# Two attention pairs of the second batch mixed as a couple, with X turned by the transfer queue

## The chip, the cores and the metric

One core of one Trainium2 chip runs the whole kernel. The metric is the device time of one execution in microseconds (us). Engines are named as in the profile: PE is TensorE (matmuls; PEld are its weight loads), DVE is VectorE, ACT is ScalarE, POOL is GpSimd, SP is SyncE, whose work here is to issue transfers in its program order.

## What is computed

Cosine attention, then a mixer that works across the sequence, then two dense layers. q, k and v have 8 batches, 12 heads, 448 positions and 64 values for each head.

```python
q_n = q / (norm(q) + 1e-6)
k_n = k / (norm(k) + 1e-6)
attn = softmax(q_n @ k_n.T / tau)
x = attn @ v                          # as (batch, 448, 768)
u = x + V.T @ (U.T @ x)               # U: 448 x 32, V: 32 x 448, over positions
out = u + relu(u @ w_ch1) @ w_ch2     # 768 -> 3072 -> 768
```

## The kernel before

**Pairs and stages.** Two heads make a pair: 6 pairs for each batch (`NP` = 6), 48 in all, counted through. Pair 10 and 11 are the last two of batch 1, pair 12 the first of batch 2. For each pair the kernel does these steps:

- Norms: q and k of a group of two pairs are loaded, squared on POOL (L243), summed on DVE (L248), rooted on ACT (L253, L254), inverted on DVE (L260, L262), and scaled to bf16 on POOL (L268).
- T: q and k are turned so that the 64 values lie on partitions. Up to pair 11 TensorE does it (`pe_T`, L297), and DVE copies the result (L302). From pair 12 on (`by_dma`, L281) SP's queue does it with a DMA transpose (L312).
- S: scores in four chunks of k's positions. Chunks 0 to 2 fill two banks each (L328), the last one half of that (L321, or `step_S3` at L332, which does the last chunks of two pairs at once). ACT takes the exponential (L350, L353).
- V: the product with v and a column of ones, in two halves (L373, L380), and the division on DVE (`divide_V`, L391, L392), which leaves X in bf16.
- Mixing: U.T X is added up over the positions, then multiplied with V, and X is added. Its result is one chunk of 128 rows of uE (even batches) or uO (odd ones), turned so that the dense layers can read it.

**Two forms of the mixing.** The one-pair form is `step_A` and `step_H`: four matmuls against U (L413) and an ACT copy (L419); four matmuls of X against the identity, which turn X into a PSUM bank (`pe_XT`, L427); one matmul of 448 columns with V (L438) into the same bank; and a DVE copy to uO or uE (L443). The couple form is used for two pairs at once. `step_XT` (L455) turns X by a DMA transpose on SP's queue as soon as it is divided. `step_A2` (L460) does both pairs' sums over U with eight matmuls of 32 columns each (L466) and one ACT copy (L470). `step_H2` (L474) multiplies with V in four matmuls of 64x64 (L480), and two DVE additions (L485) put the turned X on top. After the last pair of an odd batch, DVE copies 64 columns of uE to the end of uO (L450 or L488).

The couple form needs V on all four quarters of the partitions. `load_copies` (L159) and `place_copies` (L164) see to that, on POOL.

**Fill.** The dense layers of the batch before are cut into pieces of six matmuls: `steps_m1` (L510, 24 pieces, then a relu on ACT or DVE, L514 and L516) and `steps_m2` (L537; every four pieces one output chunk, evicted by L551, L553 or L555 and written by L561, L565). They stand in the list `fill`, and are put between the attention steps.

**The order.** Pairs 0 to 5 follow a list written out by hand (L625). From pair 6 on a loop (L791) goes over pairs n. For each, `order` lists attention steps with weights, and `spread` (L775) emits a step, then what `after` holds for that index, then its share of the fill. The dictionary `after` places the steps of the norms of later groups (L733 to L757), the loads, the DMA transposes and `place_copies`. A planner's costs (`est`) only choose ACT or DVE for some evictions. Each engine executes its instructions in the order in which they were emitted.

Pairs up to `FIRST2` = 2 * NP = 12 use the first pair of orders (L800 to L821): V of pair n - 1, then `A` and `Hs` of pair n - 1. Five pieces of fill go with each pair, and the pair that begins a batch (n = 12) gets all the rest. Then the dense layers of the batch just mixed are put into `fill`. Later pairs use the second orders (L839 to L871): V and the X transfer of pair n - 1, `A2` of a couple at the even pair after it, `H2` at the odd pair after that. Three pieces (`KEEP`) are held back from the pair that begins a batch, and run behind that `H2`.

PSUM has one bank each under the tags `ps_av` and `ps_x`. In `step_V` (L398) the second half goes to `ps_x` for pairs for which `by_dma` holds, and to `ps_av` otherwise; TensorE's turning of q and k also uses `ps_x`. For pair 12's group the squares are emitted at (9, 6) and (10, 0), sums at (10, 1) and (10, 3), the root at (10, 4), inversion and scaling at (10, 5); the numbers are pair n and index in its order.

Of the kernel before, what the change touches and what calls it, by code (L numbers as in the profile page):

```python
# [22 lines left out]
def kernel(  # L23
# [23 lines left out]
    NP = H // 2  # L47
# [233 lines left out]
    def by_dma(n):  # L281

        return n >= 2 * NP

    tp_of, sc_of = {}, {}

    def new_qkT(b, p):
# [44 lines left out]
    def step_S3(b, p):  # L332

        for i, (nm, tag) in enumerate((("av", "ps_av"), ("up", "ps_x"))):
            t = qkT[(b, p + i)]
            bank = psum.tile([128, 512], FP, name=nm, tag=tag, bufs=1)
            sc_of[(b, p + i, 3)] = bank.unsqueeze(1)
            for h in range(2):
                r, o = slice(64 * h, 64 * h + 64), 64 * (h ^ i)
                nc.tensor.matmul(out=bank[o:o + 64, 0:S], lhsT=t[r, 1, 384 + o:448 + o],  # L340
                                 rhs=t[r, 0, 0:S], start=True, stop=True)
        est.pe(0.19)
        for i in range(2):
            exp_S(b, p + i, 3)

    def exp_S(b, p, c):
        e = E[(b * NP + p) % 2]
        sc = sc_of.pop((b, p, c))
        if c == 3:
            nc.scalar.activation(out=last_of(b, p)[:, 0:S], in_=sc[:, 0, 0:S], func=AF.Exp)  # L350
            est.act(0.56)
        else:
            nc.scalar.activation(out=e[:, 2 * c:2 * c + 2, 0:S], in_=sc[:, :, 0:S], func=AF.Exp)  # L353
            est.act(0.93)

    def step_S(b, p, cs):
        for c in cs:
            pe_S(b, p, c)
            exp_S(b, p, c)
# [27 lines left out]
    def divide_V(b, p, half):  # L387
        X = X_of[(b, p)]
        av = av_of[(b, p, half)][:, 0:4 * (D + 1)].rearrange("p (i h d) -> p i h d", i=2, h=2)
        rd = work.tile([128, 4, 1], FP, name="rd", tag="rd", bufs=2)  # L390
        nc.vector.reciprocal(out=rd, in_=av.rearrange("p i h d -> p (i h) d")[:, :, D:D + 1])  # L391
        nc.vector.tensor_mul(  # L392
            X[:, 2 * half:2 * half + 2, :].rearrange("p i (h d) -> p i h d", h=2),
            av[:, :, :, 0:D],
            rd.rearrange("p (i h) o -> p i h o", h=2).to_broadcast([128, 2, 2, D]))
        est.dve(0.6)

    def step_V(b, p, half):  # L398
        if half == 1 and by_dma(b * NP + p):
            bank = psum.tile([128, 512], FP, name="up", tag="ps_x", bufs=1)  # L400
        else:
            bank = psum.tile([128, 512], FP, name="av", tag="ps_av", bufs=1)
        pe_V(b, p, half, bank)
        divide_V(b, p, half)
# [172 lines left out]
    pairs = [(b, p) for b in range(B) for p in range(NP)]  # L577
# [9 lines left out]
    def load_all(gi):  # L587
        if gi < len(groups):
            for x in ("q", "k", "v"):
                load(gi, x, nc.sync)  # L590
# [13 lines left out]
    def T(n):  # L604
        step_T(*pairs[n])

    def Sc(n, *cs):
        step_S(*pairs[n], cs)
# [121 lines left out]
    def put(n, at, fn):  # L730
        after.setdefault((n, at), []).append(fn)

    for gi in range(5, len(groups)):  # L733
        m, g = first_pair[gi], preps[gi]
        if m == NP + 2:
            at = [(NP, 1), (NP, 2), (NP + 1, 6), (NP, 5), (NP + 1, 0), (NP + 1, 1)]
            when = (NP + 1, 2)
        elif m == NP + 4:
            at = [(NP + 2, 0), (NP + 2, 1), (NP + 2, 6), (NP + 2, 4), (NP + 2, 6), (NP + 2, 7)]
            when = (NP + 3, 0)  # L740
        elif m == 2 * NP:
            at = [(m - 3, 6), (m - 2, 0), (m - 1, 0)] + [(m - 2, i) for i in (1, 3, 4)]
            when = (m - 2, 5)
        elif m == 2 * NP + 2:
            at = [(m - 2, i) for i in (0, 0, 6, 3, 4, 5)]
            when = (m - 2, 6)
        else:
            at = [(m - 3, 0), (m - 3, 0), (m - 3, 5)] + [(m - 2, i) for i in (0, 1, 2)]
            when = (m - 2, 3)

        put(*at[0], lambda g=g: g.square(0))
        put(*at[1], lambda g=g: g.square(1))
        put(*at[2], lambda g=g: g.values())
        put(*at[3], lambda g=g: g.reduce(0))
        put(*at[4], lambda g=g: g.reduce(1))
        put(*at[5], lambda g=g: g.root())
        put(*when, lambda g=g: (g.invert(), [g.scale(i, j, P_) for j in (0, 1) for i in (1, 0)]))  # L757
        if gi > 5 and m - 6 <= NP:
            put(*((NP, 3), (NP + 3, 0))[gi - 6], lambda gi=gi: load_all(gi))
        elif gi > 5:  # L760
            at = {2 * NP + 2: [(m - 4, 5), (m - 4, 6), (m - 3, 2)],
                  2 * NP + 4: [(m - 4, i) for i in (0, 2, 4)]}.get(m, [(m - 6, 4), (m - 5, 5), (m - 4, 3)])
            for x, w in zip("qkv", at):
                put(*w, lambda gi=gi, x=x: load(gi, x, nc.sync))
        if by_dma(m):
            put(m - 1, -1, lambda m=m: T(m))
            put(m - 1, 0, lambda m=m: T(m + 1))
# [2 lines left out]
    put(NP, 3, lambda: (load_w2(0, 0, 12), load_w2(0, 12, 24)))  # L770
    put(NP + 1, 2, lambda: (load_w2(1, 0, 12), load_w2(1, 12, 24)))
    put(NP + 3, 0, load_copies)
    put(NP + 5, 6, place_copies)

    def spread(n, order, nf, first=0):  # L775

# [9 lines left out]
            f(min(want - given, len(fill)))  # L786
            given = want

    FIRST2 = 2 * NP
    KEEP = 3  # L790
    for n in range(NP, NPAIR + 1):  # L791
        b, p = pairs[n] if n < NPAIR else (B, 0)
        now, nxt = n < NPAIR, n + 1 < NPAIR
        done = n > NP
        late = n > FIRST2
        for g in after.pop((n, -1), []):
            g()
        state_of["busy"] = n == NP + 1
        if not late:
            if n % 2 == 0:  # L800

                order = [
                    (1, lambda: Sc(n, 0, 1)),
                    (0, done and (lambda: V(n - 1, 0))),
                    (1, None if by_dma(n + 1) else (lambda: T(n + 1))),
                    (0, lambda: Sc(n, 3)),
                    (1, (lambda: V(n - 1, 1)) if done else None),
                    (0, done and (lambda: A(n - 1))),
                    (1, lambda: (Sc(n, 2), Sc(n + 1, 0))),
                    (1, (lambda: Hs(n - 1)) if done else None),  # L810
                ]
            else:
                order = [
                    (1, lambda: Sc(n, 1, 2)),
                    (1, lambda: V(n - 1, 0)),
                    (0, lambda: Sc(n, 3)),
                    (1, lambda: V(n - 1, 1)),
                    (1, not by_dma(n + 1) and (lambda: T(n + 1))),
                    (1, lambda: A(n - 1)),
                    (0, lambda: Hs(n - 1)),  # L820
                ]  # L821
            last = p == 0 and done
            nf = len(fill) if last else 5
            spread(n, order, nf)
            if last:
                f(len(fill))
                fill.extend(steps_m1(b - 1) + steps_m2(b - 1))
            continue

        def X2(m):  # L830
            step_XT(*pairs[m])

        def A2(m):
            step_A2(*pairs[m])

        def H2(m):
            step_H2(*pairs[m])

        if n % 2 == 0:  # L839
            order = [  # L840
                (2, now and (lambda: (step_S3(*pairs[n]), Sc(n, 0, 1)))),
                (2, lambda: V(n - 1, 0)),
                (2, lambda: (V(n - 1, 1), X2(n - 1))),
                (2, None),
                (3, lambda: (A2(n - 2), now and (Sc(n, 2), Sc(n + 1, 0)))),
                (2, not now and (lambda: H2(n - 2))),
            ]
            nf = len(fill) if not now else int(round((len(fill) - KEEP) / (1 + (-p) % NP)))
            spread(n, order, nf)
            if not now:  # L850
                f(len(fill))
                fill.extend(steps_m1(b - 1) + steps_m2(b - 1))
            continue
        Sc(n, 1, 2)
        if n - 3 >= FIRST2:
            H2(n - 3)
        for g in after.pop((n, 0), []):
            g()
        if p == 1 and n - 2 > FIRST2:
            f(len(fill))  # L860
            fill.extend(steps_m1(b - 1) + steps_m2(b - 1))
        order = [
            (2, lambda: V(n - 1, 0)),
            (2, None if n > FIRST2 + 1 else (lambda: Sc(n, 3))),
            (2, lambda: (V(n - 1, 1), X2(n - 1))),
            (2, None),
            (2, None),
        ]
        nf = int(round((len(fill) - KEEP) / (1 + (-p) % NP)))
        f(2)  # L870
        spread(n, order, nf - 2, 1)  # L871
# [37 lines left out]
```

## Time and profile before

| what | value |
|---|---|
| median of 5 runs | 583.91 us (583.34 to 587.0) |
| the profiled execution | 583.2 us, of which 581.4 are its span |
| granted clock of TensorE | 0.999 |
| TensorE's dense layers: L537, L510 (matmuls) | 233.7 us x1344; 227.2 us x1128 |
| the 24 matmuls L413 on `av`; the 48 of L427 | 2.3 us; 6.3 us |
| DMA transposes of X: queue time, to landing | 1.20 us; 2.5 us (2.4 to 4.5) |
| DMA transposes of q and k: queue time, to landing | 1.28 us (up to 2.81); 3.7 us (3.1 to 5.6) |
| DMA, mean busy share from 90 to 100 and 100 to 110 us | 1.10; 0.68 |

The span runs from the first to the last instruction, and the rest of the execution's time lies around it. The profile's groups give, for each line and shape, busy time, count and mean. Matmuls follow one another before the earlier one has ended, so a group's busy time is more than what it adds to the run; the distance between starts in the order of time is what counts. "[1.05 <-DVE X L392]" behind an instruction says that its engine sat idle for that long before it, and which instruction released it. To landing is counted from a transfer's issue until its data are there.

### The profile page before, as it was taken

What the parts mean: (1) busy time and instruction counts of PE and PEld (TensorE: products, weight loads), DVE (VectorE), ACT (ScalarE), POOL (GpSimd) and SP (SyncE); (2) the same over time, 40 slices, a digit from 0 to 9 for tenths busy, and PEclk for the clock granted to TensorE, in tenths of its full rate; (3) what the DMA queues carried; (4) which work ended last, traced back from release to release, by engine and by line L of the source; (5) the groups of instructions that cost most, each with busy time, mean ns of one, the idle gap of its engine ahead of it and who ended that gap; (6) DMA issues with size and microseconds to landing.
All of it is one profiled execution on the core that took longest, in us unless ns stands there. A gap on an engine that the chain in (4) does not pass through costs nothing.

```text
span 581.4 us, 12255 instructions
## 1 busy us (share of the span) xinstructions
PE 570.1 (98%) x5080; PEld 329.0 (57%) x5080; DVE 214.1 (37%) x462; ACT 260.6 (45%) x447; POOL 215.2 (37%) x205
## 2 busy tenths in 40 slices
PE   7999999999999999999999999999999999999997
PEld 6665556655565556555655555655555555655564
DVE  6874552433243334423324243432244332320011
ACT  5877535455433554446424455246443374214200
POOL 8754865706326146326064163253261420000000
PEclk9999999999999999999999999999999999999999
DMA  6899999646376486585465663773754640231012
GB/s 163 199 245 237 237 209 222 177 98 136 95 166 140 98 154 122 126 166 110 82 160 134 131 135 96 144 174 78 138 127 115 132 74 17 53 73 33 10 45 56
DMA packets 138585, 74.25 MB, mean 128 GB/s; under 512 B 85568, under 2 KB 138352, under 8 KB 138528
## 3 DMA queue, kind: packets, MB, share of 16 engines
q1 hardware_dynamic: 128256, 62.77, 48.8%
q0 software_dynamic: 9728, 10.18, 10.2%
q8 instruction: 40, 0.66, 0.5%
q10 hardware_dynamic: 544, 0.51, 0.3%
q14 instruction: 17, 0.14, 0.1%
HBM read 52.19 MB, written 11.01 MB: 109 GB/s over the span
## 4 chain that ended last, share of the span: by engine, by line
PE 87%; DMA 7%; DVE 2%; ACT 1%; POOL 1%; issue 1%; SPq 0%; DVEq 0%; POOLq 0%; ACTq 0%
PE mp L537 38%; PE mp L510 33%; PE sc L328 5%; DMA w_sb<-in_moe_w_ch_dram 5%; PE av L380 3%; PE up L380 2%; DMA kst<-in_k_dram 2%; PE av L373 1%; PE av L340 1%; PE up L373 1%; PE up L466 1%; DVE ss L248 1%; ACT E L353 1%; PE av L480 1%; PE tp L297 0%
## 5 line engine op out<-in xcount | busy, mean ns | idle before, releaser
L537 PE MATMUL mp<-w_sb,relu 128*128 128x384 bf16 x1344 | 233.7, 326 | 0.6 <-DMA w_sb<-in_moe_w_ch_dram 0.6
L537 PEld LDWEIGHTS <-relu 128*128 128x128 bf16 x1344 | 125.3, 98 | 89.7 <-issue 13.4
L510 PEld LDWEIGHTS <-w_sb 128*128 128x128 bf16 x1128 | 105.0, 98 | 99.5 <-issue 10.0
L514 ACT ACTIVATE relu<-mp 128x448 bf16<-128x448 f32 x161 | 87.6, 544 | 127.8 <-PE mp L510 127.8
L268 POOL TENSOR_TENSOR qk<-kst,inv 128x512 bf16<-128x512 f32 x43 | 46.0, 1070 | 242.5 <-DVE inv L262 228.3
L353 ACT ACTIVATE E<-sc 128x896 bf16<-128x896 f32 x144 | 125.1, 922 | 22.6 <-PE sc L328 21.6
L510 PE MATMUL mp<-uO,w_sb 128*128 128x448 bf16 x576 | 114.3, 353 | 0.0
L510 PE MATMUL mp<-uE,w_sb 128*128 128x448 bf16 x552 | 112.9, 353 | 0.0
L555 DVE TENSOR_TENSOR o_sb<-mp,ut 128x384 f32<-128x384 f32 x50 | 27.9, 557 | 141.4 <-PE mp L537 134.0
L248 DVE TENSOR_REDUCE ss<-sq 128x16 f32<-128x1024 f32 (+1 forms) x50 | 57.8, 1164 | 0.9 <-ACT sq L240 0.9
L268 POOL TENSOR_TENSOR qk<-qst,inv 128x512 bf16<-128x512 f32 x44 | 47.4, 1079 | 1.6 <-PE up L438 1.6
L516 DVE TENSOR_SCALAR relu<-mp 128x448 bf16<-128x448 f32 x27 | 16.9, 625 | 81.3 <-PE mp L510 80.7
L380 PEld LDWEIGHTS <-E 128*128 128x128 bf16 x1152 | 45.0, 97 | 0.0
L328 PE MATMUL sc<-qkT 64*64 64x448 bf16 x576 | 42.4, 359 | 0.6 <-ACT E L353 0.3
L243 POOL TENSOR_TENSOR sq<-kst 128x1024 f32<-128x1024 f32 (+1 forms) x23 | 42.7, 1858 | 0.1
L243 POOL TENSOR_TENSOR sq<-qst 128x1024 f32<-128x1024 f32 x21 | 39.8, 1894 | 2.9 <-DVE qk L268 2.2
L350 ACT ACTIVATE E<-av 128x448 bf16<-128x448 f32 x17 | 9.2, 541 | 47.3 <-PE up L340 47.3
L380 PE MATMUL av<-v,E 128*128 128x65 bf16 x648 | 29.1, 193 | 0.0
L276 POOL CAST v<-vst 128x1024 bf16<-128x1024 f32 (+1 forms) x25 | 25.2, 1006 | 7.7 <-DMA vst<-in_v_dram 5.8
L373 PEld LDWEIGHTS <-E 128*128 128x128 bf16 x192 | 18.1, 98 | 14.7 <-issue 0.8
L470 ACT CAST A_sb<-up 128x128 bf16<-128x128 f32 x18 | 4.8, 264 | 45.9 <-PE up L466 45.9
L391 DVE RECIPROCAL rd<-av 128x4 f32<-128x4 f32 x54 | 9.7, 179 | 42.3 <-PE av L380 42.3
(99 smaller groups left out, 351.8 us busy)
## 6 DMA issues: line engine op xcount, KB each, us to landing
out_dram<-o_sb SPq DMA_DIRECT2D x109, 96.0 KB, 2.2
w_sb<-in_moe_w_ch_dram POOLq DMA_DIRECT2D x8, 1152.0 KB, 19.1
qst<-in_q_dram SPq DMA_DIRECT2D x23, 256.0 KB, 3.9
vst<-in_v_dram SPq DMA_DIRECT2D x46, 128.0 KB, 2.9
kst<-in_k_dram SPq DMA_DIRECT2D x44, 128.0 KB, 2.7
qst<-in_q_dram SPq DMA_DIRECT2D x23, 192.0 KB, 4.0
vst<-in_v_dram SPq DMA_DIRECT2D x46, 96.0 KB, 2.7
kst<-in_k_dram SPq DMA_DIRECT2D x44, 96.0 KB, 2.7
```

The costliest lines, as they stand in the source:

```text
L243: nc.gpsimd.tensor_mul(sq[:, 0:self.nh * 4, :], self.flat(t), self.flat(t))
L248: nc.vector.reduce_sum(self.ss[:, j, 0:self.nh * 4], self.sq[j][:, 0:self.nh * 4, :], axis=AX.X)
L268: eng.tensor_mul(qks[self.gi % 2][:, j, i, :, :, :], t[:, 2 * j:2 * j + 2, :, :].rearrange("p h c d -> p c h d"), iv.unsqueeze(3).to_broad ...
L276: nc.gpsimd.tensor_copy(out=self.flat(v65[self.s])[:, :, 0:D], in_=self.flat(vst[self.s]))
L328: nc.tensor.matmul(out=sc[o:o + 64, h, 0:S], lhsT=t[r, 1, c * 128 + o:c * 128 + o + 64], rhs=t[r, 0, 0:S], start=True, stop=True)
L353: nc.scalar.activation(out=e[:, 2 * c:2 * c + 2, 0:S], in_=sc[:, :, 0:S], func=AF.Exp)
L373: nc.tensor.matmul(out=av[:, i, :, :], lhsT=last_of(b, p)[:, ic * 128:(ic + 1) * 128], rhs=vv[:, 2 * j:2 * j + 2, 3, :], start=(i == 0), s ...
L380: nc.tensor.matmul(out=av[:, i, h, :], lhsT=e[:, 2 * c + h, ic * 128:(ic + 1) * 128], rhs=vv[:, 2 * j + h, c, :], start=False, stop=(i == ...
L510: nc.tensor.matmul(out=mp, lhsT=w1_sb[:, cc, f * 128:(f + 1) * 128], rhs=u[:, cc, 0:S], start=(cc == 0), stop=(cc == CC - 1))
L514: nc.scalar.activation(out=relu[:, f, o:o + S], in_=mp, func=AF.Relu)
L537: nc.tensor.matmul(out=mp, lhsT=relu[:, f, r0:r0 + 128], rhs=w2_sb[:, f, half * HC:(half + 1) * HC], start=(f == 0), stop=(b > 0 and f == ...
L555: nc.vector.tensor_add(o.rearrange("p (k d) -> p k d", d=128), mp.rearrange("p (k d) -> p k d", d=128), ut_of[(b, half)][:, :, c, :])
```

## The change

`FIRST2` is lowered to NP + 4 = 10, and a second bound, `FIRST4` = 2 * NP + 2 = 14, is set. Pairs 11 and 12 therefore use the second orders, and pairs 10 and 11 are mixed by `step_XT`, `step_A2` and `step_H2`. Their second V half goes to the `ps_x` bank. q and k of pairs 10 and 11 are still turned by TensorE. Up to pair 13 the last chunk of the scores is done for one pair at a time; `step_S3` begins at pair 14, as before.

With the other orders the fill is dealt out differently: pair 11 has 6 pieces, pair 12 has 7, and 3 are held until pair 13, where they run behind `H2` of the couple (before: 5, 11 and 0). The steps of the norms of pair 12's group move to earlier indices, those of pair 14's by one index, and `place_copies` from (11, 6) to (11, 5), since pair 11's new order ends there.

In the order of each engine: TensorE has 6 matmuls fewer; on POOL nothing changes its place; on SP two X transfers are added, and writes, loads and q/k transfers keep their order among themselves but for the writes of the fourth and the sixth output chunk, which come before k's loads for pair 16, and behind the q/k transfers of pairs 14 and 15. On DVE the first sum of pair 12's group comes ahead of an output copy, the second ahead of a copy of qkT, and L260 and L262 ahead of pair 9's second division.

```diff
     def by_dma(n):
         return n >= 2 * NP
+    FIRST2 = NP + 4
+    FIRST4 = 2 * NP + 2
...
     def step_V(b, p, half):
-        if half == 1 and by_dma(b * NP + p):
+        if half == 1 and b * NP + p >= FIRST2:
...
         elif m == 2 * NP:
-            at = [(m - 3, 6), (m - 2, 0), (m - 1, 0)] + [(m - 2, i) for i in (1, 3, 4)]
+            at = [(m - 3, 6), (m - 3, 6), (m - 1, 0)] + [(m - 2, i) for i in (0, 1, 2)]
+            when = (m - 2, 3)
+        elif m == 2 * NP + 2:
+            at = [(m - 2, i) for i in (0, 0, 5, 2, 3, 4)]
             when = (m - 2, 5)
-        elif m == 2 * NP + 2:
-            at = [(m - 2, i) for i in (0, 0, 6, 3, 4, 5)]
-            when = (m - 2, 6)
...
-    put(NP + 5, 6, place_copies)
+    put(NP + 5, 5, place_copies)
...
-    FIRST2 = 2 * NP
...
         if n % 2 == 0:
             order = [
-                (2, now and (lambda: (step_S3(*pairs[n]), Sc(n, 0, 1)))),
+                (2, now and (lambda: (n >= FIRST4 and step_S3(*pairs[n]), Sc(n, 0, 1)))),
...
-                (2, None),
+                (2, None if n >= FIRST4 else (lambda: Sc(n, 3))),
...
-            (2, None if n > FIRST2 + 1 else (lambda: Sc(n, 3))),
+            (2, None if n > FIRST4 else (lambda: Sc(n, 3))),
```

## The prediction

> **What bounds the kernel now.** I read the page's first and fourth parts, then who TensorE waited for, then its instructions in order of time around the edit, then VectorE and the transfer queue over the same microseconds.
>
> ```profile
> PE 570.1 (98%) x5080; PEld 329.0 (57%) x5080; DVE 214.1 (37%) x462; ACT 260.6 (45%) x447; POOL 215.2 (37%) x205
> ...
> PE 87%; DMA 7%; DVE 2%; ACT 1%; POOL 1%; issue 1%; SPq 0%; DVEq 0%; POOLq 0%; ACTq 0%
> ```
>
> TensorE is busy 98% of the span and is 87% of the chain that ended last. In the windows from 90 to 130 us it is busy 10.00 of every 10 us. So an edit pays by what it takes off TensorE's own row of instructions, or by ending one of its few waits. Of those waits (11 entries, some 7 us in all, most at the start) one lies where the edit works:
>
> ```profile
> PE av L413 <- DVE X L392: 1.0, 1, 1.0
> ```
>
> TensorE in order of time (start, length; matmuls overlap, so the cost of a group is the distance between starts):
>
> ```profile
> 85.50 1.14 PE L537 MATMUL mp<-w_sb,relu 128*128 128x384 bf16 x6
> 87.68 0.38 PE L413 MATMUL av<-X,U_sb 128*128 128x128 bf16 x4 [1.05 <-DVE X L392]
> ...
> 95.73 0.39 PE L413 MATMUL av<-X,U_sb 128*128 128x128 bf16 x4
> 95.95 0.36 PE L427 MATMUL up<-ident,X 128*128 128x128 bf16 x4
> 96.15 1.14 PE L537 MATMUL mp<-w_sb,relu 128*128 128x384 bf16 x6
> ...
> 109.41 0.35 PE L438 MATMUL up<-V_sb,A_sb 128*128 128x448 bf16 x1
> 109.60 3.09 PE L537 MATMUL mp<-w_sb,relu 128*128 128x384 bf16 x18
> ```
>
> This is the one-pair form of pairs 9, 10 and 11: sums over U (L413), X turned by identity (L427), the product with V (L438). The same work as a couple is seen one batch later:
>
> ```profile
> 133.38 0.30 PE L466 MATMUL up<-X,U_sb 128*32 128x128 bf16 x8
> 133.61 0.57 PE L328 MATMUL sc<-qkT 64*64 64x448 bf16 x8
> 134.12 3.58 PE L510 MATMUL mp<-uO,w_sb 128*128 128x448 bf16 x18
> 137.62 0.57 PE L328 MATMUL sc<-qkT 64*64 64x448 bf16 x8
> 138.03 0.35 PE L480 MATMUL av<-V_sb,A_sb 64*64 64x448 bf16 x2
> ...
> 138.32 2.44 PE L510 MATMUL mp<-uO,w_sb 128*128 128x448 bf16 x12
> ```
>
> And VectorE ahead of the wait at 87.68, with the two sums (L248) of pair 12's group before the division (L391, L392) that TensorE waits for:
>
> ```profile
> 84.15 1.21 DVE L248 TENSOR_REDUCE ss<-sq 128x16 f32<-128x1024 f32 x1
> 85.28 0.68 DVE L302 COPY qkT<-tp 128x1024 bf16<-128x1024 bf16 x1
> 85.87 1.21 DVE L248 TENSOR_REDUCE ss<-sq 128x16 f32<-128x1024 f32 x1
> 87.00 0.17 DVE L391 RECIPROCAL rd<-av 128x4 f32<-128x4 f32 x1
> 87.20 0.42 DVE L392 TENSOR_TENSOR X<-av,rd 128x256 bf16<-128x256 f32 x1
> 87.73 0.18 DVE L260 TENSOR_SCALAR ss<-ss 128x32 f32<-128x32 f32 x1
> 87.95 0.35 DVE L262 RECIPROCAL inv<-ss 128x32 f32<-128x32 f32 x1
> ```
>
> **The couple on TensorE.** Removed for each of two pairs: L413 and L427, 95.73 to 96.15 = 0.42 us, and L438, 109.41 to 109.60 = 0.19; together 1.22. Added once: L466 and L480. The scores L328 take 0.50 (133.61 to 134.12) and, after a run of fill, a gap of 0.10 ahead of them (L547 takes 0.26 instead of 0.17 where L328 follows). From the end of the fill to the end of L466 and L328 it is about 0.82 (fill from 129.89, 18 at 0.189, ends at 133.29; next fill at 134.12), so L466 costs 0.22. L328 with L480 takes 137.62 to 138.32 = 0.70, so L480 costs 0.20. Sum 0.42. Saved: 1.22 - 0.42 = 0.80 us, all on the path. Fill that moves from pair 12 to 11 and 13 keeps its number; nothing of TensorE's order changes from the first L510 of batch 1 on.
>
> [...] The trace has L427 at 0.20 us a pair on the engine that sets the end, and the transfer of a whole X at 1.20 us of queue and 2.5 to landing (4.5 at most), off it. So the question is cover.
>
> **Cover of the two transfers.** New on the queue: two X transfers, 1.2 us each, in order. In the trace of before SP is nearly solid from 91.7 to 111.7. I put them in: writes of the second output chunk 91.3 to 92.5, two q/k transfers (3.8 us) to 96.3, four v loads to 99.1, X of pair 10 to 100.4 (ready at 95.9), third chunk's writes and q loads to 103.0, fourth's writes to 104.2, X of pair 11 (ready near 102.9) issued at 104.2, landed by 106.7, at the worst seen 108.7. Its reader, the L485 addition, comes after L480 at about 108.9. Then three fill pieces run (0.98 each) to 112.0, and L510 asks for pair 10's and 11's rows last of six, at 112.8 and 113.0. So each addition (0.6 us on VectorE, replacing two L443 copies of 0.62) is covered, and the cost is 0; uncovered, each us past 112.4 costs one. Behind the X transfers wait k and v loads for pairs 16 and 17, wanted some 20 us later, and the q/k transfers of pairs 14 and 15 (issued 114.61 before, wanted at 124.8; I get 113 to 116): 0.
>
> **Sums sooner.** Order on VectorE becomes: first sum right after L443 at 81.9 (GpSimd's square of q ends at 80.5), second sum at 84.15 as the first was, L302 at 85.28, L260 and L262, then the division. L260 comes 1.86 us after the second sum's start (85.87 to 87.73: sum, two ScalarE steps): 86.01. Add 0.57 for L260 and L262, then 0.20 and 0.42 for the division: 87.20 against 87.62. TensorE's wait of 1.05 shrinks by 0.42; what remains of it is L260 and L262 ahead of the division. Exponentials of pair 10's last chunk go behind the root, 0.8 us later, read at 92.6: 0. Scaling on GpSimd starts 1.7 sooner, but its transfers stay behind the second chunk's writes: 0. The copies of V (GpSimd) come before L480 instead of behind pair 10's L438: their loads, issued at 77.0, take 17.7 at the most, so they end near 96: 0. The sums of pair 14's group are moved by an index only and land between divisions and additions with about 1 us free: 0, or up to 0.6 if they push the L485 pair. V(10) and V(11) taking the spare bank: it was emptied more than 2 us before each time: 0.
>
> **Sum.** 0.80 + 0.42 = 1.22. The profiled execution took 583.2 (span 581.4, 1.8 around it); it becomes 582.0. The median of five is 583.91 with two runs at 583.34 and 583.37; I add 0.4 for where a median falls: 582.4.
>
> **Rivals.** All start from 583.6. (a) Whole wait gone: if L260 is held up by ScalarE, it still comes first in VectorE's order, so this needs the division to be sooner than I make it; 1.05 + 0.80 = 1.85, 581.8. Against it stands the written order. [...] (c) Slower: the second X transfer comes late. Its place is the solid stretch of the queue. If it left only where the queue was free before, 111.7, and took the longest landing, 4.5, it lands at 116.2 and the addition ends at 116.8, 3.8 after the sixth L510 asks: 583.6 - 1.22 + 3.8 = 586.2. It costs from a landing past 112.4, beats the gain past 113.6, and makes over 0.5% past 116.5. Against it: 4 us of margin, and in batch 3 the same step has its X transfer issued at 241.86 for a use at 245.82, with no wait. (d) The change doesn't do what it says: the distances between starts may hold weight loads that the neighbours would need anyway, so that the six matmuls fewer save nothing, and the moved sums give way to another wait: 583.6.
>
> **How the numbers follow.** Likeliest 0.62 (582.4, own range 581.8 to 583.2), (a) 0.10, (b) 0.13, (c) 0.10, (d) 0.05. The range goes from 581.0, a little under (a) for the spread of runs, to 585.6, into (c). A measurement of this kernel tells about 0.5%, 2.9 us, from no change. The most that can be saved is 1.85 us, so faster by over that needs something not in the trace: 0.03. Slower by over it needs the upper part of (c), or stalls in several places: 0.09. Within it: 0.88.
>
> **What would show it.** Right: L466 and L480 near 105 and 108.6, the wait at L413 near 87.3 with 0.6 instead of 1.05, the first L510 of batch 1 near 112.0 instead of 113.29, and no wait of TensorE on L485. Wrong: L510 waiting for uO; the X transfer of pair 11 issued after 108; L328 of pair 12 waiting for its q/k transfer at 98.5; or the start of L510 moved but not the end, which would mean that a later wait takes up what was won.

## The result, and the profile after

| | before | after |
|---|---|---|
| median | 583.6 us (71 runs, 582.53 to 587.0) | 582.0 us (36 runs, 581.03 to 584.94) |
| profiled execution, its span | 583.2, 581.4 | 581.8, 580.0 |

The ratio is 0.9972, with a 95% interval from 0.9964 to 0.9979: 1.6 us less, between 1.2 and 2.1. Ratios leave disturbed runs out, so they need not be the quotient of the medians. Run again later, beside some of its own variants, the changed kernel took 582.17 (14 runs; 0.9983, 0.9973 to 0.9992). Forecast were 582.4 for the median and 582.0 for the profiled execution.

The first and fourth parts of the page after:

```profile
PE 569.3 (98%) x5074; PEld 328.1 (57%) x5074; DVE 213.5 (37%) x461; ACT 261.1 (45%) x447; POOL 215.2 (37%) x205
...
PE 87%; DMA 7%; DVE 2%; ACT 1%; SPq 1%; POOL 1%; issue 0%; DVEq 0%; POOLq 0%
```

TensorE is still what bounds the kernel, with six matmuls fewer. Its instructions in order of time, at the places shown of before (three lines lower in the code: L416 is L413, L430 L427, L469 L466, L483 L480, L513 L510, L540 L537):

```profile
85.69 1.14 PE L540 MATMUL mp<-w_sb,relu 128*128 128x384 bf16 x6
87.32 0.38 PE L416 MATMUL av<-X,U_sb 128*128 128x128 bf16 x4 [0.49 <-DVE X L395]
...
105.39 0.30 PE L469 MATMUL up<-X,U_sb 128*32 128x128 bf16 x8
105.61 0.57 PE L331 MATMUL sc<-qkT 64*64 64x448 bf16 x8
106.12 1.15 PE L540 MATMUL mp<-w_sb,relu 128*128 128x384 bf16 x6
...
108.34 0.57 PE L331 MATMUL sc<-qkT 64*64 64x448 bf16 x8
108.74 0.35 PE L483 MATMUL av<-V_sb,A_sb 64*64 64x448 bf16 x2
...
109.03 3.10 PE L540 MATMUL mp<-w_sb,relu 128*128 128x384 bf16 x18
111.97 0.33 PE L550 MATMUL mp<-ident,uE 128*128 128x128 bf16 x3
112.14 2.43 PE L513 MATMUL mp<-uO,w_sb 128*128 128x448 bf16 x12
```

The wait for pair 9's division is 0.49 instead of 1.05. The couple's two steps are at 105.39 and 108.74, and the first L513 of batch 1 starts at 112.14 instead of 113.29. VectorE ahead of the first of these lines and around the couple's additions:

```profile
84.35 1.21 DVE L248 TENSOR_REDUCE ss<-sq 128x16 f32<-128x1024 f32 x1
85.47 0.68 DVE L305 COPY qkT<-tp 128x1024 bf16<-128x1024 bf16 x1
86.21 0.18 DVE L260 TENSOR_SCALAR ss<-ss 128x32 f32<-128x32 f32 x1
86.42 0.35 DVE L262 RECIPROCAL inv<-ss 128x32 f32<-128x32 f32 x1
86.69 0.12 DVE L394 RECIPROCAL rd<-av 128x4 f32<-128x4 f32 x1
86.84 0.42 DVE L395 TENSOR_TENSOR X<-av,rd 128x256 bf16<-128x256 f32 x1
...
109.14 0.62 DVE L488 TENSOR_TENSOR uO<-av,XT 128x448 bf16<-128x448 f32 x1 [0.23 <-PE up L483]
109.68 0.61 DVE L488 TENSOR_TENSOR uO<-up,XT 128x448 bf16<-128x448 f32 x1
```

The additions were released by TensorE's L483, not by a transfer: X of pair 11 had landed. The transfer queue (SP) shows by how much:

```profile
92.62 4.53 SPq L315 DMA_TRANSPOSE qkT<-qk  x2
...
99.98 1.22 SPq L461 DMA_TRANSPOSE XT<-X  x1
...
105.28 2.04 SPq L461 DMA_TRANSPOSE XT<-X  x1
```

It was issued at 105.28, about a us later than I had placed it (q/k took 4.53 on the queue, not 3.8), and took 3.5 us to landing, so it landed near 108.8. Its addition starts at 109.68. TensorE would wait for that addition only if it started after about 112.5: the sixth L513, which reads its row, starts near 113.1, and the addition takes 0.61.

**Where the time went.** A profile is one execution, and its load of w2 differs from one to the next: TensorE waited 0.60 us for it at 79.98 before, 0.82 after, in the experiments between nothing and 2.13. So I measure the stretch behind that wait: from the start of pair 8's step with V (L438, L441) to pair 14's first scores (`step_S3`, L340, L343). It took 43.84 us before, 42.47 after: 1.37 less. In each of the 18 later couples the start of `step_H2` stands 1.16 or 1.17 sooner in the whole execution's time, the first (138.03 against 136.86) as the last (516.20 against 515.03). Nothing later took it up or added to it. (0.20 of the 1.37 was lost to the longer wait for w2.) Behind the stretch all the kernels below are alike but one, that in which TensorE turns all X: from pair 14's first scores to the start of the last output addition they take 452.32 or 452.33 us. So a profiled time differs by the stretch, by what lies ahead of it (80.34 to 83.47 us, a spread most of which is the wait for w2), and by the last writes (some 4.0 to 4.3 us).

### The profile page after: what moved, and what is told of

The parts are those of the page before. It is cut to its first block, busy times and chain, and to the rows that moved or that the text cites. A ratio compares the mean times of both kernels' runs of the same rounds, so it can differ in the third digit from the quotient of the medians.

```text
span 580.0 us, 12249 instructions
## 1 busy us (share of the span) xinstructions
PE 569.3 (98%) x5074; PEld 328.1 (57%) x5074; DVE 213.5 (37%) x461; ACT 261.1 (45%) x447; POOL 215.2 (37%) x205
## 4 chain that ended last, share of the span: by engine, by line
PE 87%; DMA 7%; DVE 2%; ACT 1%; SPq 1%; POOL 1%; issue 0%; DVEq 0%; POOLq 0%
PE mp L540 38%; PE mp L513 33%; PE sc L331 5%; DMA w_sb<-in_moe_w_ch_dram 5%; PE av L383 3%; PE up L383 2%; DMA kst<-in_k_dram 2%; PE av L343 1%; PE av L376 1%; PE up L376 1%; ACT E L356 1%; PE up L469 1%; PE av L483 1%; DVE qk L268 0%; DVE ss L248 0%
## 5 line engine op out<-in xcount | busy, mean ns | idle before, releaser
L540 PE MATMUL mp<-w_sb,relu 128*128 128x384 bf16 x1344 | 233.6, 326 | 0.8 <-DMA w_sb<-in_moe_w_ch_dram 0.8
L540 PEld LDWEIGHTS <-relu 128*128 128x128 bf16 x1344 | 125.3, 98 | 90.5 <-issue 14.0
L513 PEld LDWEIGHTS <-w_sb 128*128 128x128 bf16 x1128 | 105.1, 98 | 99.1 <-issue 9.3
L513 PE MATMUL mp<-uO,w_sb 128*128 128x448 bf16 x576 | 114.2, 352 | 0.0
L513 PE MATMUL mp<-uE,w_sb 128*128 128x448 bf16 x552 | 112.9, 353 | 0.0
L331 PE MATMUL sc<-qkT 64*64 64x448 bf16 x576 | 42.3, 359 | 0.6 <-ACT E L356 0.3
L394 DVE RECIPROCAL rd<-av 128x4 f32<-128x4 f32 x52 | 9.3, 178 | 46.2 <-PE av L383 46.2
```

Of the source, the lines that this page charges most:

```text
L331: nc.tensor.matmul(out=sc[o:o + 64, h, 0:S], lhsT=t[r, 1, c * 128 + o:c * 128 + o + 64], rhs=t[r, 0, 0:S], start=True, stop=True)
L513: nc.tensor.matmul(out=mp, lhsT=w1_sb[:, cc, f * 128:(f + 1) * 128], rhs=u[:, cc, 0:S], start=(cc == 0), stop=(cc == CC - 1))
L540: nc.tensor.matmul(out=mp, lhsT=relu[:, f, r0:r0 + 128], rhs=w2_sb[:, f, half * HC:(half + 1) * HC], start=(f == 0), stop=(b > 0 and f == ...
```

## Experiments

"Stretch" is the one just defined, "wait" that of TensorE at pair 9's L413 or L416. The stretch holds only this one couple, so where all X is turned by TensorE it shows one of 19. The variants were run in three groups, each with before beside it; its medians there were 583.67, 583.37 and 583.63.

| kernel | median, us | ratio to before (95%) | wait | stretch, us |
|---|---|---|---|---|
| before | 583.6 | 1 | 1.05 | 43.84 |
| changed | 582.0 | 0.9972 (0.9964 to 0.9979) | 0.49 | 42.47 |
| changed, again | 582.17 | 0.9983 (0.9973 to 0.9992) | 0.5 | 42.47 |
| sums alone | 582.98 | 0.9982 (0.9969 to 0.9995) | 0.49 | 43.31 |
| couple alone | 582.03 | 0.9965 (0.9953 to 0.9978) | 1.05 | 43.03 |
| sums later | 584.74 | 1.0019 (1.0005 to 1.0032) | 2.2 | 44.20 |
| this couple's X turned by TensorE | 583.15 | 0.9987 (0.9976 to 0.9998) | 0.49 | 43.10 |
| all X turned by TensorE | 594.04 | 1.0185 (1.0165 to 1.0204) | 0.5 | 43.10 |
| second X transfer late | 588.21 | 1.0086 (1.0060 to 1.0111) | 0.49 | 47.69 |
| second X transfer half as late | 583.27 | 0.9998 (0.9990 to 1.0007) | 0.5 | 43.67 |
| no kept fill | 582.38 | 0.9983 (0.9976 to 0.9990) | 0.49 | 42.82 |
| division first | 581.56 | 0.9959 (0.9948 to 0.9970) | none | 42.18 |
| division first, q/k transfer early | 581.53 | 0.9972 (0.9962 to 0.9983) | none | 42.30 |

**Sums alone.** The kernel before, with

```diff
-            at = [(m - 3, 6), (m - 2, 0), (m - 1, 0)] + [(m - 2, i) for i in (1, 3, 4)]
-            when = (m - 2, 5)
+            at = [(m - 3, 6), (m - 3, 6), (m - 1, 0)] + [(m - 2, i) for i in (0, 1, 2)]
+            when = (m - 2, 3)
```

> The kernel before with one thing changed: the steps of pair 12's group (squares, sums, root, inversion) at the indices that the changed kernel gives them. No couple. My theory (two separate terms): the wait of TensorE ahead of L413 in pair 10's turn falls from 1.05 us to about 0.5, so the run is 0.5 us shorter than before, and TensorE's order is untouched. Rival 1 (the sums did nothing alone, the wait fell because the couple's order shifted things): wait stays at 1.05, 0 us. Rival 2 (all of the gain is the sums): 1.2 to 1.6 us shorter.

The stretch is 0.53 shorter and the wait 0.49. In the profile's waits of TensorE:

```profile
PE mp L537 <- DMA w_sb<-in_moe_w_ch_dram: 2.1, 1, 2.1
...
PE av L413 <- DVE X L392: 0.5, 1, 0.5
```

The first line shows why whole profiled times can't be compared here: this execution took 584.27 us, with 1.5 more of that load's wait than before.

**Couple alone.** The changed kernel, with pair 12's `at` and `when` as before:

```diff
-            at = [(m - 3, 6), (m - 3, 6), (m - 1, 0)] + [(m - 2, i) for i in (0, 1, 2)]
-            when = (m - 2, 3)
+            at = [(m - 3, 6), (m - 2, 0), (m - 1, 0)] + [(m - 2, i) for i in (1, 3, 4)]
+            when = (m - 2, 5)
```

> The changed kernel with pair 12's steps back at their old indices. Theory: the wait of 1.05 us at L416 (pair 9's sums over U) is back, the couple's saving of 0.80 us stays; 0.8 us shorter than before, 0.5 to 0.6 longer than the changed kernel; distance from that L416's start to the first L513 of batch 1 the same 24.8 us as in the changed kernel. Rival 1 (the couple pays for itself only with the earlier sums, since its exponentials and divisions come late otherwise): no gain over before. Rival 2 (all of the gain is the couple): as the changed kernel, 1.2 to 1.6 shorter than before.

The wait is back at 1.05, and the stretch is 0.81 shorter than before. From that L416 (88.75) to the first L513 (113.56) are 24.81 us, in the changed kernel 24.82. 0.53 and 0.81 make 1.34, of 1.37. But the median is that of the whole change, 582.03 against 582.0, where 0.5 more was expected. Its interval, 1.3 to 2.7 us less than before, leaves the stretch's 0.81 out. Behind the stretch nothing differs, so what it has beyond 0.81, if it is more than chance, must lie ahead of it or in the last writes; other executions than the profiled one leave no trace in which to look. By the medians alone the sums would be worth nothing, so I made the wait large enough to be seen in them.

**Sums later.** The changed kernel, with both sums, the root and the inversion ahead of pair 9's second division:

```diff
-            at = [(m - 3, 6), (m - 3, 6), (m - 1, 0)] + [(m - 2, i) for i in (0, 1, 2)]
+            at = [(m - 3, 6), (m - 3, 6), (m - 1, 0)] + [(m - 2, i) for i in (2, 3, 3)]
```

> The changed kernel with both sums of pair 12's group later on DVE: behind the copy of qkT, so that two sums, the root on ACT and L260 and L262 all stand ahead of pair 9's second division. TensorE's order is untouched. Theory (that wait goes one for one into the time): the wait at L416 grows from 0.49 to about 2.2 us, the run is about 1.7 us longer than the changed kernel, the same as before within 0.3. Rival (the wait is taken up by slack elsewhere, which would explain why the couple alone had the same median as the whole change): as the changed kernel.

The wait is 2.2 us, the stretch 1.73 longer than the changed kernel's; the median is 2.6 above the changed kernel run beside it, and by the ratios 2.1. That it is slower than before (1.0005 at the least) was not expected in full; the excess over 1.73 lies within the two intervals. The wait goes into the time, and is not taken up. In the stretch, then, two terms of about 0.8 and 0.5 stand; what share each has of the median remains unresolved below half a us.

**X of this couple turned by TensorE.** The changed kernel; `step_XT` does nothing for pairs 10 and 11, and `step_H2` does this for them (written out here for this couple alone; the others keep their form):

```diff
+        for i in range(2):
+            for c in range(4):
+                nn = 128 if c < 3 else 64
+                nc.tensor.matmul(out=ups[i][:, c * 128:c * 128 + nn], lhsT=X_of[(b, p + i)][:, c, :],
+                                 rhs=ident[:, 0:nn], start=(c == 0), stop=False, skip_group_check=True)
...
-                                 rhs=V_sb[rows, :], start=True, stop=True)
+                                 rhs=V_sb[rows, :], start=False, stop=True, skip_group_check=True)
...
-            nc.vector.tensor_add(u_of(b)[:, p + i, 0:S], ups[i][:, 0:S], xt[:, 0:S])
+            nc.vector.tensor_copy(u_of(b)[:, p + i, 0:S], ups[i][:, 0:S])
```

> The changed kernel, but X of pairs 10 and 11 is turned by TensorE again (eight matmuls against the identity into the two banks, just ahead of the four with V, and two DVE copies instead of two additions); the sums over U stay the couple's. Theory: 2 x 0.20 = 0.40 us longer than the changed kernel, to which up to 0.1 for a switch of tiling in front of L480's step may come, so 0.4 to 0.5; no wait. Rival 1 (the transfers cost somewhere as much as they save): as the changed kernel or shorter. [...]

The stretch is 0.63 longer, more than the 0.4 to 0.5. TensorE in order of time (L489 turns, L494 is the product with V):

```profile
110.66 0.57 PE L331 MATMUL sc<-qkT 64*64 64x448 bf16 x8
111.17 0.37 PE L489 MATMUL av<-ident,X 128*128 128x128 bf16 x4
111.37 0.36 PE L489 MATMUL up<-ident,X 128*128 128x128 bf16 x4
111.66 0.38 PE L494 MATMUL av<-V_sb,A_sb 64*64 64x448 bf16 x2
...
111.98 3.10 PE L555 MATMUL mp<-w_sb,relu 128*128 128x384 bf16 x18
```

The turn is 0.40, from 111.17 to about 111.57. In the changed kernel L331 and L483 together took 0.69 (108.34 to 109.03); here, torn apart, 0.51 + 0.32, and 0.09 lies ahead of L494. Either the four matmuls with V cost only 0.20 because they follow the scores, which are 64x64 as they are, or they are slower here because they add to banks that the turn has just written. The last couple of the changed kernel tells the two apart. It has no scores ahead of its L483, and nothing has been turned into its banks:

```profile
512.00 3.10 PE L540 MATMUL mp<-w_sb,relu 128*128 128x384 bf16 x18
515.03 0.38 PE L483 MATMUL av<-V_sb,A_sb 64*64 64x448 bf16 x2
...
515.35 2.12 PE L540 MATMUL mp<-w_sb,relu 128*128 128x384 bf16 x12
```

The 18 fill matmuls, 0.163 apart, end near 514.94. L483 follows after a gap of 0.09 and costs 0.32, as here. So adding to the turned banks costs nothing that can be seen, and what the four matmuls lose here, 0.41 instead of 0.20, is their place behind the scores.

**All X turned by TensorE.** The same for all 19 couples.

> The changed kernel with every couple's X (19 couples, 38 pairs) turned by TensorE again ahead of the matmuls with V, with DVE copies instead of additions; no X transfers at all. Theory: 19 x 0.40 = 7.6 us longer than the changed kernel, up to 19 x 0.5 = 9.5 with a switch of tiling each, so that a turn by transfer is worth 0.2 to 0.25 us a pair where it is covered. Rival (fewer transfers free SP's queue and the DMA engines, which gives some of it back): under 6.

The median is 12.0 above the changed kernel's (of four runs; the profiles differ by 11.4, or 11.5 with the wait for w2 taken out), more than the 7.6 to 9.5 expected. In the profile each couple from the second to the 18th adds 0.62, within 0.01, as this one couple did. The last, which has no scores to be torn from, adds only 0.39:

```profile
526.03 0.36 PE L489 MATMUL av<-ident,X 128*128 128x128 bf16 x4
526.23 0.36 PE L489 MATMUL up<-ident,X 128*128 128x128 bf16 x4
526.51 0.38 PE L494 MATMUL av<-V_sb,A_sb 64*64 64x448 bf16 x2
...
526.83 2.12 PE L555 MATMUL mp<-w_sb,relu 128*128 128x384 bf16 x12
```

From 526.03 to 526.83 are 0.80 us, where the changed kernel had 0.41. So the turn is worth 0.4 by itself, and 0.6 where it stands between the scores and the product with V. Nothing came back from the freed queue, whose mean DMA busy share from 130 to 330 us was 0.51 instead of 0.62: the step from couple to couple stays the same.

**Second X transfer late.** The changed kernel, with X of pair 11 issued behind ten loads:

```diff
-                (2, lambda: (V(n - 1, 1), X2(n - 1))),
+                (2, lambda: (V(n - 1, 1), n != 2 * NP and X2(n - 1))),
...
+    put(2 * NP, 4, lambda: step_XT(*pairs[2 * NP - 1]))
```

> The changed kernel with one transfer later on SP's queue: X of pair 11 is issued behind k's and v's loads for pair 16 and q's for pair 18, instead of ahead of them. Nothing else moves. Theory (cover up to a landing near 112.4, then one for one): issued at 112 to 113, landed 2.5 us later at 114.5 to 115.5, its L488 addition ends at 115 to 116 while TensorE asks for that row at 113.1; a wait of TensorE of 2 to 3 us on the addition, the run 2 to 3 us longer than the changed kernel, about 1 longer than before. Rival (the turned X is not on the path, or the wait is taken up by slack later): as the changed kernel.

TensorE's order of time, and below it three stretches with busy times, the granted clock (after the instruction counts), DMA share and GB/s:

```profile
112.50 1.11 PE L513 MATMUL mp<-uO,w_sb 128*128 128x448 bf16 x5
117.03 2.36 PE L513 MATMUL mp<-uO,w_sb 128*128 128x448 bf16 x7 [3.42 <-DVE uO L488]
...
120.08 1.69 PE L513 MATMUL mp<-uO,w_sb 128*128 128x448 bf16 x6
121.80 1.30 PE L513 MATMUL mp<-uO,w_sb 128*128 128x448 bf16 x6
```

```profile
116.00:118.00 2.00, 0.97 (x4) 0.43 (x4) 0.92 (x2) 0.55 (x1) 2.00 (x2) 0.87 0.89 178
118.00:120.00 2.00, 2.00 (x17) 1.25 (x16) 0.00 (x0) 0.54 (x1) 0.16 (x1) 0.50 0.93 186
120.00:122.00 2.00, 2.00 (x14) 1.01 (x12) 0.61 (x2) 0.19 (x1) 0.00 (x0) 0.78 0.95 185
```

Five L513 run, the sixth, which needs pair 11's row, waits: issued at 112.60, the transfer let the addition start at 116.34. The sixth comes 3.58 us late (112.50 plus five at 0.19, against 117.03). But the stretch is 5.22 longer, where 2 to 3 were expected. The other 1.6 us are seen in the second fence: TensorE's granted clock is 0.50 from 118 to 120, and six L513 take 1.69 instead of 1.30. In slices of 0.4 us the clock is still 1.00 from 117.0, 0.59 from 117.4, 0.50 from 117.8 and 0.89 again from 120.8: about 3.3 us at half clock, which cost half of that. So this gap of 3.42 us cost 3.58 by itself and 1.6 more at the lower clock behind it.

**Half as late.** The same transfer behind eight loads instead of ten:

```diff
+            if m == 2 * NP + 4:
+                put(2 * NP, 4, lambda: step_XT(*pairs[2 * NP - 1]))
```

> The changed kernel with the X transfer of pair 11 half as late as in the late one: behind k's and v's loads for pair 16 but ahead of q's for pair 18. Theory: issued near 111.3, landed at 113.7 to 115, the addition 0.6 later, TensorE waits 1 to 2 us on it; its clock stays at full, as the gap is well under the 3.4 us after which it fell, and the run is longer by the wait alone, 1 to 2 us over the changed kernel. Rival (any wait of over a us there lowers the clock): 1 to 2 us more than the wait.

```profile
112.24 1.11 PE L513 MATMUL mp<-uO,w_sb 128*128 128x448 bf16 x5
114.39 1.48 PE L513 MATMUL mp<-uO,w_sb 128*128 128x448 bf16 x7 [1.04 <-DVE uO L488]
```

The addition started at 113.71, held by the transfer (issued at 110.98, 2.6 us to landing), and the sixth L513 is 1.20 late (112.24 plus 0.95, against 114.39). The stretch is 1.20 longer, the clock 1.00 throughout, and the time that of before (0.9998). So the gap of 1.04 us cost 1.20, about its length, and the clock's price came with the gap of 3.42 only; nothing between the two was tried.

**No kept fill.** Pair 12 gets all its ten pieces, and L513 follows the couple at once:

```diff
-            nf = len(fill) if not now else int(round((len(fill) - KEEP) / (1 + (-p) % NP)))
+            nf = len(fill) if not now or n == 2 * NP else int(round((len(fill) - KEEP) / (1 + (-p) % NP)))
```

> The changed kernel without the three pieces of fill kept for pair 13: pair 12 gets ten pieces, and L513 of batch 1 follows the couple's L483 at once. Theory: the additions end about 1.3 us after L483 starts and the sixth L513 asks for pair 11's row 1.2 us after it, so a wait of 0.1 to 0.3 us, if the copy of 64 columns behind the additions is not waited for; 1.0 to 1.2 us if it is. Rival (the kept pieces carry the gain, since the transfer of X is what they cover): 2 us or more.

The sixth L513 is late by 0.36 (113.80, five after 112.49; 0.1 to 0.3 were expected) and the stretch is 0.35 longer. The three kept pieces hide only that much; without them the transfer itself is still not waited for (the first addition, at 112.59, was released by L483, and the second follows at 113.14), since pair 12's fill, longer by three pieces, now runs ahead of the additions.

**Division first.** The changed kernel, with L260 and L262 behind pair 9's second division:

```diff
-            when = (m - 2, 3)
+            when = (m - 2, 4)
```

> The changed kernel with inversion and scaling of pair 12's group one index later, so that on DVE the second division of pair 9 comes ahead of L260 and L262. TensorE's order is untouched. Theory: the remaining wait of 0.49 at L416 falls to under 0.1, the first L513 of batch 1 starts 0.45 earlier (111.7 instead of 112.14), and nothing takes it up later: 0.4 to 0.5 us shorter than the changed kernel, about 2 shorter than before. Rival (the wait is owed to the sum and the copy of qkT ahead of it, not to L260 and L262): the wait stays at 0.3 or more, gain under 0.2.

The wait is gone, and the stretch 0.29 shorter than the changed kernel's, not 0.45: 0.21 comes back at pair 12's scores, which now wait for q and k:

```profile
98.31 0.57 PE L331 MATMUL sc<-qkT 64*64 64x448 bf16 x8 [0.21 <-DMA qkT<-qk]
```

Of all kernels run it has the lowest ratio, 0.9959 (0.9948 to 0.9970), 2.1 us under before by the medians of its group. Its interval overlaps the changed kernel's, so the medians don't part the two; the stretch does, by 0.29.

**Division first, q/k transfer early.** Pair 12's transfer is also put ahead of the second chunk's writes:

```diff
-            put(m - 1, -1, lambda m=m: T(m))
+            put(*((m - 2, 7) if m == 2 * NP else (m - 1, -1)), lambda m=m: T(m))
```

> The version with pair 9's division ahead of L260 and L262, and, besides, pair 12's q/k transfer ahead of the second output chunk's two writes on SP's queue. Theory: both waits, 0.49 at L416 and the 0.21 at L331 that followed it, are gone; the first L513 of batch 1 is 31.5 us behind the L540 piece ahead of pair 8's L441 (changed kernel 31.96); 0.4 to 0.7 us shorter than the changed kernel, 1.9 to 2.3 shorter than before. Rival (the transfer's landing is set by the loaded DMA engines, not by its place): the 0.2 wait stays.

My theory fell here. The transfer was issued at 88.61 instead of 92.11. Of these 3.5 us 0.86 is only the wait for w2, which this execution didn't have; counted from pair 8's L441 (80.34 here, 81.20 there) it was issued 2.6 us earlier. Pair 12's scores waited for it all the same, 0.33 at 97.57: it took 8.9 us to landing, against 6.2 in its old place, and counted from L441 both landed after some 17.1 to 17.2 us. The stretch is 42.30, no better. The mean DMA busy share from 88 to 98 us is 1.21 in the changed kernel, and an earlier place in this stretch of the queue didn't bring an earlier landing. What held it up wasn't tried.

**The changed kernel again**, beside the last variants:

> The changed kernel itself, on the same chip as its variants, since the variants differ from it by a few tenths: 1.2 to 2.1 us shorter than before, by its interval. What the wait for w2 at L540 near 80 us (0.6 before, 0.8 in the changed kernel's profile, 2.1 in that of the sums alone) is in this execution shows how far a profile's own time can be moved by that load.

Its stretch is 42.47, to the hundredth that of the first profile, with a w2 wait of 0.64. The stretch repeats far better than a whole time does.

## Why the prediction was right

- *The couple on TensorE, 0.80.* Measured 0.81 with the couple alone. Right, and for the reason given: it was read from the row of the couple one batch later, 0.22 for L466 and 0.20 for L480. A smaller saving, rival (b), was not shown: the wait fell from 1.05 to 0.49, and the couple's 0.81 came in full. But turned by TensorE the same couple costs 0.63 where the rows of the one-pair form said 0.40. The extra 0.23 came where the turn parts the matmuls with V from the scores ahead of them (0.41 instead of 0.20); the last couple, which has no scores there, pays 0.39.
- *Turning X: TensorE or transfer.* TensorE for all couples cost 12.0 us by the medians, 11.5 by the profiles: here TensorE is the bound (busy 98% of the span), and the transfer is covered (no wait on L488). I had this on the right side, but too small (0.20 a pair; 0.31 measured).
- *Cover of the transfers, 0.* Right: no wait on L488. Placed a us early (104.2 against 105.28), within the margin. The turning points hold too: I had put the first cost at a landing past 112.4 and the loss of the whole gain at 113.6, and the half-late run landed near 113.6, lost 1.20 of the stretch's 1.37 and took the time of before. The full price of rival (c) was mis-sized: 586.2, or 2.6 over before, for a landing at 116.2. A landing near 116.2 made the stretch 3.85 longer than before's, and the median of four runs 588.21; the half clock behind the gap (0.50 for about 3.3 us, 1.6 us in time) was missing in it.
- *Sums sooner, 0.42.* Measured 0.53 in the stretch and 0.56 in the wait. L260 started at 86.21, just where forecast once the 0.20 of the w2 wait is added. From there to L394 it took 0.48, not 0.57, and L394 took 0.12 instead of 0.17. Why these small steps follow more closely in this order was not tried.
- *Sums of pair 14's group, scaling, V's copies, bank: 0.* Right, but for one thing that was nearer than said: the weight load of pair 12's L331 already waits 0.3 for the q/k transfer in the changed kernel, hidden under TensorE's work. One more half us saved ahead of it, and it shows (division first).
- *Sum.* 1.22 against 1.37 in the stretch and 1.6 in the ratio (1.2 to 2.1). The 0.4 added for where a median falls was not needed in full: the profiled execution took 581.8 and the median is 582.0.

What stays open: the medians give the couple alone as much as the whole change. The stretch says otherwise by 0.56, and the intervals of couple alone and of division first leave their own stretches' gains (0.81 and 1.66) out. Behind the stretch the kernels are alike, so the medians' own differences must arise ahead of it or in the last writes, but no run here ties the median below half a us.

## What to carry to other kernels

Where one engine sets the end, count an edit by the distance between starts on that engine, the gaps between matmuls of different form included (0.09 ahead of L483 in the last couple), and try small matmuls of one form next to each other (four of 64x64 cost 0.20 us behind others, 0.41 with the gap behind 128x128 ones). A slower way on another engine was free here as long as its landing stayed ahead of its reader (no wait for a landing near 108.8, 1.20 us more for one near 113.6, 5.22 for one near 116.2): work out that margin, and the point at which the loss begins, from the queue's own order of issues. And when a saving is smaller than what a load at the start moves from run to run, measure a stretch between two instructions behind that load, and check that the lead is the same in every later part.

## What the runs showed of the hardware

A wait of TensorE of 1.04 us cost 1.20 and left the granted clock at 1.00. One of 3.42 cost 3.58; from 0.4 us after the restart on the granted clock was 0.50 for about 3.3 us, which cost 1.6 more. A DMA transpose issued 2.6 us earlier, in a stretch with a mean DMA busy share of 1.21 in the changed kernel, landed no earlier: 8.9 us from issue instead of 6.2. Turning one X by four matmuls against the identity cost 0.31 us of TensorE between the scores and the product with V, and 0.20 where no scores stood ahead. Four 64x64 matmuls cost 0.20 us behind others of that form, and 0.32 with a gap of 0.09 ahead of them behind 128x128 ones.
